# Chunk 8 of a retention kernel turned by VectorE and ScalarE instead of TensorE

## The chip, the cores and the metric

The kernel runs on one core of a Trainium2 chip. The metric is the device time of one execution in microseconds (us). The kernel before took 932.46 us (median of 3 runs, 931.74 to 933.03). A core has five engines that work side by side, each through a queue of its own: TensorE (PE; its weight loads are listed as PEld), VectorE (DVE), ScalarE (ACT), GpSimd (POOL) and SyncE (SP, which here only issues transfers).

## The reference: what is computed

Retention without a normalisation, for 8 batches, 8 heads, 576 positions and 64 channels per head, and then a feed-forward layer with a squared ReLU over the 4608 tokens of 512 channels:

```python
def _attn_ref(q, k, v):
    scores = scale * np.matmul(q, k.transpose(0, 1, 3, 2))
    gamma = 1.0 - 2.0 ** (-5.0 - np.arange(H))
    rel = pos[:, None] - pos[None, :]
    Dmat = np.where(rel >= 0, gamma[:, None, None] ** rel[None, :, :], 0.0)
    return np.matmul(scores * Dmat[None], v)

x = attn_out.transpose(0, 2, 1, 3).reshape(B * S, H * D)
h = np.maximum(x @ w_in, 0.0)          # w_in: 512 x 2048
out = h * h @ w_out                    # w_out: 2048 x 512
```

All of it is in fp32. The weights come as 64-bit numbers and are rounded to fp32 on the chip.

## The kernel before

**Tiles and stages.** The 4608 tokens are cut into 36 chunks of 128 (C) and 9 blocks of 512 (TOK), four chunks to a block. The decay is split into a factor of q and one of k/v, so a chunk needs its scores, a mask, the product with v, and a running state u that is carried from half chunk to half chunk (64 rows; 9 halves make a sequence). The results go to xT, transposed, which the feed-forward layer reads. The first layer of block 0 is plain products (`first_in`, 16 steps of 8 matrix products each); the blocks after it use a scheme of seven products (`ffn_in`). The second layer follows once all chunks are done.

**The order is written by hand.** The main loop runs i from 5 to 36. In turn i it finishes chunk i - 1 (`whole(i - 1)`, which also makes the scores of chunk i), prepares the transposed q and k of a later chunk, issues loads, and runs some steps of the feed-forward layer (`ffn(i - 1)`). While block 0 lasts (i = 5 to 8), `ffn` runs 3 steps, called a, b and c here. Each has a few copies (`move`), the six instructions of rounding one piece of weights (`convert(6)`: L227, L231, L238, L241 and L244 on VectorE, L235 on ScalarE between them), one entry of the list `flips`, and one `first_in`, whose eviction is L683 on ScalarE and whose squaring L685 is issued one step later, before the next L683. Engines take their work in the order of issue.

**Two ways to transpose q and k of a chunk.** Up to chunk N_TURN - 1, `turn` does it on TensorE: `turn_in` makes 16 transposes (L445) into two PSUM banks, `turn_out` copies these to the tile qk (L454, two copies of 128 x 512, here both on ScalarE). From chunk N_TURN on, `flip` does it in advance: two entries of `flips` with one VectorE transpose each in squares of 32 (L416; k first, then q), the second of which also puts 16 copies of 32 x 256 into the list `moves`. `move(count)` then issues up to `count` of these on ScalarE (L431), which puts the squares in their places. A move of block 0's turns can be issued from the step after the one that listed it.

**What whole(i) asks of ScalarE.** After the first products of the state (first group of L568) ScalarE copies the state out of PSUM (`grown`, L501). TensorE goes on with half of the scores of chunk i + 1 (L480) and the carry products (L609, 32 of them, or 16 where a sequence begins within the chunk), and then adds to the same PSUM bank (second group of L568). At its end ScalarE copies the result to xT (`x_out`, L550) and the state again (L501).

**Scaling.** q and v of each chunk are scaled in place by GpSimd (`scale_q`, L396, and `scale_v`, L495), in the order of issue. How far ahead scale_q runs depends on N_TURN too (the last lines of the loop below). Buffers: 3 tiles of q, 5 of k, 4 of v, 3 of qk, 2 of flip, 3 PSUM banks for `first_in`.

```python
    for i in range(N_EARLY + 1, N_CH + 1):
        move(C, i)
        whole(i - 1)
...
        if i + 1 < N_TURN:
            turn(i + 1, (0, 0))
...
        if N_TURN <= i + 2 < N_CH:
            flip(i + 2)
        ffn(i - 1)
        for j in range(n_scaled[0], min(i + (4 if i > N_TURN - 4 else 3), N_CH)):
            n_scaled[0] += 1
            scale_q(j, nc.gpsimd)
```

Of the kernel before, what the change touches and what calls it, by code (L numbers as in the profile page):

```python
# [41 lines left out]
def kernel(  # L42
# [290 lines left out]
    def convert(count):  # L333
        for _ in range(count):
            f = next(w_in_steps, None)
            f and f()
# [61 lines left out]

    N_TURN = 9
    ps_t = [None]
    moves = []

# [7 lines left out]
    def flip(i):  # L412
        t = work2.tile([128, 4, 2, HP, 32], F32, tag="flip", name="flip")

        def one(j):
            nc.vector.transpose(t[:, :, j, :, :], loaded[i][j].rearrange("s (p e) (d a) -> s (e d) p a", e=2, d=2))  # L416

        def two():
            one(0)
            to = new_qk(i)  # L420
            for b in range(C // 32):
                for g in range(4):

                    moves.append((i, done[0] + (1 if steps[0][0] == 0 else 2), to[32 * g:32 * g + 32, :, :, 32 * b:32 * b + 32], t[32 * b:32 * b + 32, g, :, :, :]))

        flips.extend([lambda: one(1), two])

    def move(count, i=N_CH):

        while moves and count and moves[0][0] <= i and (moves[0][1] <= done[0] or count == C):  # L430
            nc.scalar.copy(*moves.pop(0)[2:])  # L431
            count -= 1
# [23 lines left out]
    def turn(i, engines=(0, 1)):  # L456
        turn_in(i)
        turn_out(i, engines)
# [338 lines left out]
    def step():  # L797
        n, f, *args = steps.pop(0)
        done[0] += 1
        f(*args)  # L800
        for _ in range(2 if len(transfers) > 2 else 1):
            if transfers and ahead[0] > QUIET:
                transfers.pop(0)[1]()
# [9 lines left out]
    def ffn(i):  # L813

        if steps and steps[0][0] == 0:

            for _ in range((N_W1 - N_EARLY) * C // TOK):
                move(4)
                convert(6)
                for f in flips[:1]:  # L820
                    f()
                del flips[:1]
                step()
            return
        count = N_MP * NP * C // TOK
        while steps and count:
            held[0] = count <= 1

            due = sum(m[0] <= i + 2 for m in moves)
            move(max(2, min(4, -(-due // (count - 1)))) if count > 1 else 0)  # L830
            ahead[0] = count
            busy[0] = len(flips) > 0
            for f in flips[:1]:
                f()
            del flips[:1]
            step()
            count -= 1
        held[0] = busy[0] = False
        ahead[0] = N_DF
# [7 lines left out]
    def loads(i):  # L847
        if i + 3 < N_CH:
            load(i + 3, "qk")
        if i + 2 < N_CH:  # L850
            load(i + 2, "v")
# [63 lines left out]
# [3 lines that stand above are left out]
        if i == N_EARLY + 1:  # L918
            convert(4)
        if i + 1 < N_TURN:  # L920
            turn(i + 1, (0, 0))
        if i + 1 < N_CH:
            scale_v(i + 1)
        loads(i)
# [6 lines that stand above are left out]
# [296 lines left out]
```

## Time and profile before

| | before |
|---|---|
| median of 3 runs | 932.46 us (931.74 to 933.03) |
| the profiled execution, its own time | 931.4 us |
| its span, first to last instruction | 929.7 us |
| granted TensorE clock | 0.999 |
| turn i = 6 (chunk 5 finished), turn i = 7, turn i = 8 | 53.88 to 67.14, 67.14 to 80.41, 80.41 to 93.03 us |
| transposes of TensorE, L445 | 144, the last ones at 69.3 to 69.9 us |
| copies of them, L454 | 15 on ScalarE (591 ns median), 3 on VectorE (691 ns) |
| VectorE transposes, L416 | 54, 702 ns median, from 73.1 us on |
| copies into place, L431 | 432, 402 ns median, from 77.6 us on |

A profile is taken of one execution; the time of that execution is somewhat longer than the span of its instructions. "Busy" is the time in which an engine has an instruction running. A line of a timeline has the start, the duration, the engine, the line of the kernel, the operation, what is written and read with its shape, and how many such instructions it sums up; in square brackets stands the idle time of the engine before it and what ended it. A line of the chain of waits in order of time has start, duration, engine and line of one piece of the work that leads to the end. Durations of matrix products overlap[...], so they don't add up; the distance between starts does.

### The profile page before, as it was taken

To read this page: it belongs to the slowest core of one execution; us is meant where nothing else is said; L and a number is where in the kernel's file an instruction comes from. 1 tells how busy PE (TensorE), PEld (TensorE's weight loads), DVE (VectorE), ACT (ScalarE), POOL (GpSimd) and SP (SyncE) were. 2 spreads that over 40 slices of the span, in tenths; PEclk is the share of its full clock that TensorE was granted. 3 is DMA by queue.
4 is the path that set the end of the run, shared out by engine and by line. 5 is a ranking of instruction groups with operands and counts; after the bars stand their busy time and mean duration, and the time that the engine had idled before them with its cause. 6 is when DMAs were issued, how large, how long until landed. Compare 5 with 4: busy or idle time off the path is not lost.

```text
span 929.7 us, 21073 instructions
## 1 busy us (share of the span) xinstructions
PE 922.7 (99%) x8548; PEld 830.3 (89%) x8548; DVE 756.2 (81%) x1215; ACT 346.4 (37%) x788; POOL 84.3 (9%) x84
## 2 busy tenths in 40 slices
PE   8999999999999999999999999999999999999998
PEld 7654888888888888888888899999999999999997
DVE  5888798888898888979876587878888888877887
ACT  3457767667676676676711110000000000000000
POOL 3322111121111111211000000000000000000000
PEclk9999999999999999999999999999999999999999
DMA  9998657678666785784379996566666575465523
GB/s 223 223 258 231 169 150 200 165 212 267 166 182 182 261 216 146 224 267 140 115 255 345 381 334 194 145 165 197 175 165 195 151 209 156 116 177 138 151 85 68
DMA packets 297152, 181.29 MB, mean 195 GB/s; under 512 B 194112, under 2 KB 270016, under 8 KB 296160
## 3 DMA queue, kind: packets, MB, share of 16 engines
q1 hardware_dynamic: 292064, 178.81, 66.4%
q10 hardware_dynamic: 4928, 1.08, 0.6%
q8 instruction: 67, 1.10, 0.5%
q14 instruction: 29, 0.24, 0.1%
q0 software_dynamic: 64, 0.07, 0.0%
HBM read 109.39 MB, written 70.52 MB: 194 GB/s over the span
## 4 chain that ended last, share of the span: by engine, by line
PE 98%; DVE 1%; issue 0%; POOL 0%; ACT 0%; POOLq 0%; DVEq 0%
PE h_b L717 18%; PE o_b L1063 17%; PE h_a L717 12%; PE h_c L717 12%; PE o_c L1063 12%; PE o_a L1063 12%; PE h_ps L677 6%; PE x_ps L574 3%; PE sc_ps L480 2%; PE x_ps L609 1%; PE u_ps L568 1%; PE idle_ps L845 0%; PE t_ps L445 0%; PE sc_ps L509 0%; PE x_ps L535 0%; DVE room L513 0%
## 5 line engine op out<-in xcount | busy, mean ns | idle before, releaser
L717 PE MATMUL h_b<-room,w 128*128 128x256 f32 x768 | 181.5, 379 | 0.0
L431 ACT COPY qk<-flip 32x256 f32<-32x256 f32 x432 | 173.8, 402 | 6.7
L717 PEld LDWEIGHTS h_b<-room,w 128*128 128x128 f32 x768 | 145.8, 190 | 20.0 <-DVE room L736 0.2
L717 PE MATMUL h_a<-room,w 128*128 128x256 f32 x512 | 123.9, 385 | 0.0
L717 PE MATMUL h_c<-room,w 128*128 128x256 f32 x512 | 121.0, 379 | 0.0
L717 PEld LDWEIGHTS h_c<-room,w 128*128 128x128 f32 x512 | 97.3, 190 | 13.2
L717 PEld LDWEIGHTS h_a<-room,w 128*128 128x128 f32 x512 | 95.0, 190 | 13.7
L1063 PE MATMUL o_b<-room,w 128*128 128x192 f32 x496 | 90.7, 326 | 0.0
L1076 ACT COPY r<-o_a 128x192 f32<-128x192 f32 x28 | 8.9, 319 | 209.4 <-PE o_a L1063 209.4
L1063 PEld LDWEIGHTS o_b<-room,w 128*128 128x128 f32 x496 | 82.3, 190 | 0.0
L724 DVE SCALAR_TENSOR_TENSOR room<-room 128x512 f32<-128x512 f32 x96 | 67.2, 700 | 3.3
L396 POOL TENSOR_TENSOR q_ld<-q_ld,dv 128x512 f32<-128x512 f32 x34 | 37.8, 1113 | 286.2 <-DMA q_ld<-in_q_dram 240.7
L1063 PE MATMUL o_a<-a,w 128*128 128x192 f32 x352 | 62.6, 326 | 0.0
L1063 PE MATMUL o_b<-s,w 128*128 128x192 f32 x336 | 61.5, 326 | 0.0
L1063 PE MATMUL o_c<-s,w 128*128 128x192 f32 x336 | 61.5, 326 | 0.0
L1063 PE MATMUL o_c<-room,w 128*128 128x192 f32 x336 | 61.5, 326 | 0.0
L677 PE MATMUL h_ps<-room,w 128*128 128x512 f32 (+1 forms) x152 | 57.7, 532 | 0.6 <-DVE w L244 0.5
L1063 PEld LDWEIGHTS o_a<-a,w 128*128 128x128 f32 x352 | 58.1, 190 | 0.1
L1063 PE MATMUL o_a<-room,w 128*128 128x192 f32 x320 | 56.9, 326 | 0.0
L1063 PEld LDWEIGHTS o_b<-s,w 128*128 128x128 f32 x336 | 55.8, 190 | 0.0
L1063 PEld LDWEIGHTS o_c<-s,w 128*128 128x128 f32 x336 | 55.8, 190 | 0.0
L1063 PEld LDWEIGHTS o_c<-room,w 128*128 128x128 f32 x336 | 55.8, 190 | 0.0
(117 smaller groups left out, 1412.6 us busy)
## 6 DMA issues: line engine op xcount, KB each, us to landing
g_dram<-room SPq DMA_DIRECT2D x164, 256.0 KB, 3.8
a<-g_dram SPq DMA_DIRECT2D x30, 512.0 KB, 5.8
room<-g_dram SPq DMA_DIRECT2D x28, 512.0 KB, 5.1
w_dram<-w SPq DMA_DIRECT2D x28, 448.0 KB, 4.4
w<-w_dram SPq DMA_DIRECT2D x7, 1792.0 KB, 9.6
q_ld<-in_q_dram SPq DMA_DIRECT2D x64, 128.0 KB, 4.1
w<-in_moe_w_in_dram SPq DMA_DIRECT2D x16, 512.0 KB, 6.0
w<-in_moe_w_out_dram SPq DMA_DIRECT2D x64, 128.0 KB, 3.4
```

Source lines behind the costliest of these rows:

```text
L396: engine.tensor_tensor(t, t, dv[:, heads, at:at + 1].to_broadcast(list(t.shape)), op=ALU.mult)
L431: nc.scalar.copy(*moves.pop(0)[2:])
L480: nc.tensor.matmul(st[i]["sc"][e][rows(h), hp, :], lhsT=st[i]["kT"][rows(e), hp, t], rhs=st[i]["qT"][rows(e), hp, t], start=True, stop=Tru ...
L568: return [lambda hp=hp, e=e, b=b: nc.tensor.matmul(u[rows(e), hp, :], lhsT=loaded[i][1][rows(h), 2 * hp + e, :], rhs=st[i]["vs"][rows(h), ...
L574: return [lambda hp=hp, e=e, b=b: nc.tensor.matmul(x_at(hp, e, b, h), lhsT=s["vs"][rows(h), head(hp, e), :], rhs=s["ret"][rows(h), e, hp, ...
L609: m = nc.tensor.matmul(x_at(hp, e, b, h), lhsT=u[rows(e), hp, :], rhs=s["qT"][rows(e), hp, CH * h:CH * h + CH], start=clears(b, e), stop=F ...
L677: nc.tensor.matmul(p, lhsT=w[:, c, :], rhs=xT[0][:, c, :].rearrange("p (h t) -> p h t", h=2)[:, lo:hi, at[0]:at[1]], start=(c == 0), stop= ...
L717: nc.tensor.matmul(p[:, mm, :], lhsT=w[:, c, :], rhs=xs[n][right][:, c, :], start=(j in OPENS and mm == 0 and c == 0), stop=(j in CLOSES a ...
L724: nc.vector.scalar_tensor_tensor(t, t, 0.0, t, op0=ALU.max, op1=ALU.mult)
L1063: nc.tensor.matmul(p, lhsT=w_out[j][:, m, WO_SLOT[right], :], rhs=s["lefts"][left][:, m, :], start=(i in OPENS and m == 0), stop=(i in CLO ...
L1076: nc.scalar.copy(r[:, 0, LEFT], p)
```

## The change

N_TURN goes from 9 to 8: chunk 8 is now transposed by `flip(8)` in turn i = 6 (its two VectorE transposes stand in steps a and b, its first copies in step c) instead of by `turn(8)` in turn i = 7. In the turns of block 0 up to 5 copies are issued in a step where it was 4. As the bound of the scaling loop also reads N_TURN, scale_q(8) is issued in turn 5 instead of turn 6.

```diff
-    N_TURN = 9
+    N_TURN = 8
...
             for _ in range((N_W1 - N_EARLY) * C // TOK):
-                move(4)
+                move(5)
                 convert(6)
                 for f in flips[:1]:
                     f()
```

## The prediction

> **What bounds the kernel now.** I read the busy shares and the chain of waits on the page first, then the chain in order of time around the first block, then a table of engine time by turn of the main loop, and last the timelines of ScalarE (ACT), VectorE (DVE) and TensorE (PE) there.
>
> ```profile
> PE 922.7 (99%) x8548; PEld 830.3 (89%) x8548; DVE 756.2 (81%) x1215; ACT 346.4 (37%) x788; POOL 84.3 (9%) x84
> ...
> PE 98%; DVE 1%; issue 0%; POOL 0%; ACT 0%; POOLq 0%; DVEq 0%
> ```
>
> PE sets the end: whatever delays or frees PE goes into the time almost one to one. ACT is at 37% over the whole span, but that is no guide here, since it is idle after 480 us. The place of the change is 54 to 93 us, turns i = 6, 7 and 8:
>
> ```profile
> core 0: us, PE busy (x) PEld busy (x) DVE busy (x) ACT busy (x) POOL busy (x), PEclk, DMA share, GB/s
> 53.88:67.14 13.26, 13.26 (x169) 7.11 (x168) 12.05 (x18) 7.58 (x15) 3.32 (x3) 1.00 0.96 267
> 67.14:80.41 13.27, 13.27 (x170) 7.11 (x169) 9.27 (x18) 8.99 (x18) 2.02 (x2) 1.00 0.92 261
> 80.41:93.03 12.62, 12.62 (x154) 6.53 (x153) 11.87 (x17) 10.31 (x23) 5.18 (x6) 1.00 0.82 195
> ```
>
> PE is full in all three turns, and the two turns that hold 16 transposes are 0.65 us longer than the third. The chain in order of time has the same:
>
> ```profile
> 69.28 0.06 PE u_ps L568 x3
> 69.34 0.64 PE t_ps L445 x16
> 69.98 10.50 PE h_ps L677 x24
> ...
> 82.54 0.06 PE u_ps L568 x3
> 82.60 10.50 PE h_ps L677 x24
> ```
>
> The transposes of chunk 8 (L445) stand bare between two other pieces of PE work: 0.64 us.
>
> The third thing is how close PE is to waiting for ACT. In whole(i), ACT copies the running state out of PSUM (`grown`, L501), and PE may add to that bank again (second group of L568) only when the copy is done. Timeline, whole(4) and then whole(6):
>
> ```profile
> 41.37 0.41 PE L609 MATMUL x_ps<-qk,u_sb 64*64 64x64 f32 x16
> 41.38 0.37 ACT L501 COPY u_sb<-u_ps 128x256 f32<-128x256 f32 x1
> 41.90 0.27 PE L568 MATMUL u_ps<-v_ld,k_ld 64*64 64x64 f32 x2
> ...
> 67.89 0.65 PE L609 MATMUL x_ps<-qk,u_sb 64*64 64x64 f32 x32
> 67.91 0.37 ACT L501 COPY u_sb<-u_ps 128x256 f32<-128x256 f32 x1
> 68.42 0.27 PE L568 MATMUL u_ps<-v_ld,k_ld 64*64 64x64 f32 x2
> ```
>
> whole(4) has 16 carry products (L609) where whole(6) has 32, yet L568 follows the start of whole after 1.27 us in both (40.63 to 41.90, 67.15 to 68.42) and 0.14 to 0.15 us after the end of L501. So in whole(4) PE does wait for the copy, and with 32 products the slack is some 0.05 us at most. If ACT comes to L501 late, PE stands still by the same amount.
>
> And ACT comes to it just in time in turn i = 8, after the first four copies of chunk 9 (timeline):
>
> ```profile
> 76.67 0.70 DVE L416 STREAM_TRANSPOSE flip<-q_ld 128x512 f32<-128x512 f32 x1
> 77.08 0.60 ACT L683 ACTIVATE room<-h_ps 128x512 f32<-128x512 f32 x1 [1.65 <-PE h_ps L677]
> 77.58 1.63 ACT L431 COPY qk<-flip 32x256 f32<-32x256 f32 x4
> 79.23 0.72 ACT L235 ACTIVATE w<-w,exp_bias 128x512 uint32<-128x512 uint32 x1
> 79.86 0.61 ACT L685 ACTIVATE room<-room 128x512 f32<-128x512 f32 x1
> 80.51 0.60 ACT L683 ACTIVATE room<-h_ps 128x512 f32<-128x512 f32 x1
> 81.17 0.37 ACT L501 COPY u_sb<-u_ps 128x256 f32<-128x256 f32 x1
> ```
>
> L683 at 80.51 starts exactly when its products are done (the first of that turn was 3.74 us after PE began, and each step is 3.43 us: 69.91 + 3.74 + 6.86 = 80.51). L501 at 81.17 is also on time. There is nothing left over.
>
> [...] L501 never passes an L683 or an L431 issued before it. [...] L431 has 402 ns[...]. [...] Here L231 takes 1.28 us beside the GpSimd scaling at 56.80 us, and 0.42 us otherwise; the transposes L416 (671 to 705 ns, all 54) show no such growth.
>
> **The change part by part.**
>
> *PE, turn 7.* turn(8) is gone: 16 transposes, -0.64 us, all on the path. Their PSUM banks are not short (L677 shows no wait).
>
> *ACT and DVE.* Two copies L454 (1.09 us) leave turn 7. Two L416 enter turn 6 (steps a and b of three; 0.62 us each from start to next start, as at 76.67 to 77.30). 16 L431 enter, 0.41 us each: 5 in step c of turn 6, 5 in a, 5 in b and 1 in c of turn 7. Then chunk 9's copies follow with 4 in c of turn 7, 5, 5 and 2 in turn 8, and 3 of chunk 10. So turns 6, 7, 8 get 5, 15, 15 copies where they had 0, 4, 12. In turn 7 one step on ACT is now 5 x 0.41 + L235 0.63 + L685 0.52 + L683 0.55 (start to next start) = 3.76 us, against 3.43 us of PE.
>
> *GpSimd.* The condition i > N_TURN - 4 lets scale_q(8) be issued one turn earlier, ahead of scale_v(7). Its q was issued by SP at 46.58 us and lands in about 4 us, so the 1.06 us at 56.80 moves to about 52. Nothing is added; the 0.86 us it cost L231 moves into turn 5, where DVE has 0.56 us idle before L491. I take DVE to be about 0.5 us earlier in turn 6 for it (bounds 0 to 0.86).
>
> *Turn 6.* DVE ended step b at 63.49 us. With two transposes (+1.24) and 0.5 earlier, the flip of chunk 8 ends near 64.2 (64.9 without the gain). ACT is free after L683 of step b at 63.82 + 0.53 = 64.35. Five copies: L235 at 66.42, L685 at 67.05, L683 at 67.57 (before: 67.25), L501 at 68.13 instead of 67.91. PE stalls 0.2; if the flip comes at 64.9 and is seen by 65.05, it is 0.9. I take 0.3.
>
> *Turn 7*, counted from x_out (L550) of whole(6): two copies L501/L550 0.8; five L431 to 2.86; L235, L685, L683 start at 2.86, 3.49, 4.03 (PE is ready at 3.7); five L431 from 4.6; L235 of step b at 6.66, ends 7.38. DVE's third pass of step b (L241) has been waiting for that L235: L241 7.41, L244 8.14, and only behind these in its queue the transpose of chunk 9's q, 8.75 to 9.45. ACT, which did L683 and the last copy of chunk 8 by 8.85, waits for it: four L431 from 9.55, L235 11.2, L685 11.85, L683 12.4, L501 12.95. In the trace of before that L501 is 11.26 us after PE began h_ps, so 11.2 from x_out. Late by 1.75 us (1.55 to 2.0, from the start-to-start gaps 0.5 to 0.66 after L683 and 0.75 to 0.87 after L550), and PE stalls by it in whole(7).
>
> *Turn 8 and after.* L501 isn't called in whole(8) in this place, for chunk 8's second half ends a sequence; five copies without L235 in steps b and c (2.06 + 0.63 + 0.55 = 3.2 us) fit beside 3.43 of PE. From turn 9 on the instructions are the same, but for three fewer copies left. Weights: step c of turn 7 needs a piece converted in its step a, which ends near 5.0, and PE comes to it at 6.8; covered. The SP queue's loads and the stores of g come up to 2 us later and are needed 8 us or more later; 0.
>
> *Sum:* -0.64 + 0.3 + 1.75 = +1.4 us. Against the profiled execution: span 929.7 to 931.1, its own time 931.4 to 932.8. The median of the runs shown is 932.46, 1.1 above that execution; with the same difference 933.9.
>
> **Rivals.** An effect of 0.2% (1.86 us) is about what a measurement of this kernel can tell from no change.
>
> (A) Forecast: both stalls as worked out, net +0.7 to +1.8. For it: the two copies L501 on time to 0.05 us. Chance 0.44.
>
> (B) The flip of chunk 8 comes late in turn 6, because DVE isn't freed by the earlier scaling or is held by another GpSimd pass in step a or b. Place: the L431 of step c, turn 6. Price: each 0.1 us past 64.35 is 0.1 us of stall; at 65.05 it gives -0.64 + 0.9 + 1.75 to 2.0 = +2.0 to 2.3, 934.5 to 934.8. It decides from copies starting after 64.8. For it: DVE has 12.05 us busy of 13.26 there. Against: part of that is overlap of records, and it idles 1.94 us before L491 at 69.16. Chance 0.36; and 0.07 for slower still, where lateness reaches a bank or a load that I count as covered.
>
> (C) The stalls aren't passed on, PE having other work to pull ahead: -0.64, 931.8. Against it stands whole(4). Chance 0.05.
>
> (D) ACT is late by its own queue only, as chunk 9's flip isn't behind L244 in effect: then L501 comes 0.7 to 1.1 us earlier in turn 7, net about +0.5, 933.0. Chance 0.05. That the change doesn't do what it says I hold excluded: turn is guarded by i + 1 < N_TURN alone. A gain of over 1.86 us has no source in the trace, 0.03 for what I don't see.
>
> **Numbers.** No measurable change: A, C, D, 0.54; slower 0.43; faster 0.03. Range 932.3 to 935.6: D's end to B with 1 us of scatter between runs (931.74 to 933.03). The likeliest case alone: 933.1 to 934.3.
>
> **What would show it.** t_ps x128 instead of x144 matrix products; 448 L431; L445 absent near 69 us; in the waits of PE two stalls before the second group of L568, near 68.4 (0.2 to 0.9) and near 81.7 us (about 1.75), each 0.14 us after an L501; in turn 7 ACT without idle time before L683, and DVE idle 2 us before L241 of step c. Wrong would be: L501 on time in whole(7), or PE going on without it, or a loss after 95 us.

## The result, and the profile after

The changed kernel takes 933.18 us (median of 20 runs, 932.58 to 934.92), the kernel before, run beside it, 931.76 us (20 runs, 931.31 to 933.03): ratio 1.0016, 95% interval 1.0010 to 1.0023. That is 1.4 us slower, as worked out. The interval lies above 1, so the loss is real, and it is smaller than the 0.2% that the prediction took as the least effect that can be told. The span of the profiled execution goes from 929.7 to 931.0 us.

The times fall in two groups: 16 runs from 932.58 to 933.65 us and 4 from 934.23 to 934.92. The profiled execution (932.70 us) is of the lower group, so what follows is the account of that one.

The same view as before, engine time by turn (each turn counted from the first matrix product of its whole):

```profile
core 0: us, PE busy (x) PEld busy (x) DVE busy (x) ACT busy (x) POOL busy (x), PEclk, DMA share, GB/s
53.91:67.18 13.27, 13.27 (x170) 7.11 (x169) 11.46 (x19) 9.01 (x19) 3.12 (x2) 1.00 1.01 269
67.18:80.13 12.95, 12.85 (x154) 6.66 (x153) 10.30 (x16) 10.97 (x25) 2.12 (x2) 1.00 0.94 262
80.13:94.45 14.32, 12.85 (x153) 6.66 (x153) 12.40 (x18) 11.93 (x28) 5.27 (x5) 1.00 0.75 169
```

Turn 7 is 0.32 us shorter than before (12.95 against 13.27), turn 8 is 1.70 us longer (14.32 against 12.62) and TensorE isn't busy for 1.47 us of it. So 0.64 us were saved, and 0.32 and 1.70 lost; whole(8) begins 1.42 us later than before (94.45 against 93.03), and after it nothing more is lost: the span ends 1.3 us later.

The timeline of TensorE at the second group of L568, where both losses are, with ScalarE's copy of the state ahead of it, in whole(6) and in whole(7):

```profile
68.28 0.36 ACT L501 COPY u_sb<-u_ps 128x256 f32<-128x256 f32 x1
68.78 0.27 PE L568 MATMUL u_ps<-v_ld,k_ld 64*64 64x64 f32 x2
...
82.65 0.36 ACT L501 COPY u_sb<-u_ps 128x256 f32<-128x256 f32 x1
83.11 0.27 PE L568 MATMUL u_ps<-v_ld,k_ld 64*64 64x64 f32 x2 [1.47 <-POOL v_ld L495]
```

whole(6) began at 67.19 us and whole(7) at 80.14 us (first L568), so the second group comes after 1.59 and 2.97 us where it was 1.27: stalls of 0.32 and 1.70 us. In both it follows the end of L501 by 0.10 to 0.14 us.

But the profile names another culprit for the second: L495, the scaling of a v by GpSimd. So does the chain of waits in order of time, which leaves TensorE there and runs back for tens of us through loads that bound nothing:

```profile
76.72 4.30 DMA v_ld<-in_v_dram
81.02 0.07 issue
81.09 1.31 POOL v_ld L495
82.40 0.71 issue
83.11 0.27 PE u_ps L568 x2
```

The reader should be wary of the 0.71 us of "issue" between the supposed releaser and the released: from the end of L501 to the second group of L568 it was 0.10 to 0.15 us in every case shown, here and in the prediction. By order of issue this L495 is also that of chunk 9's v, which whole(7) doesn't read. Which of the two it was is the first thing that the experiments decide.

How ScalarE came to be late in turn 7 (timeline; the lines of VectorE that it waits for are put between):

```profile
69.67 0.59 ACT L550 COPY room<-x_ps 128x512 f32<-128x512 f32 x1 [1.03 <-PE x_ps L574]
...
74.42 2.07 ACT L431 COPY qk<-flip 32x256 f32<-32x256 f32 x5
76.52 0.72 ACT L235 ACTIVATE w<-w,exp_bias 128x512 uint32<-128x512 uint32 x1
77.28 0.69 DVE L241 SCALAR_TENSOR_TENSOR w<-w,w 128x512 f32<-128x512 f32 x1 [0.43 <-ACT w L235]
78.00 0.69 DVE L244 SCALAR_TENSOR_TENSOR w<-w,w 128x512 uint32<-128x512 uint32 x1
78.61 0.70 DVE L416 STREAM_TRANSPOSE flip<-q_ld 128x512 f32<-128x512 f32 x1
...
79.35 1.65 ACT L431 COPY qk<-flip 32x256 f32<-32x256 f32 x4 [0.68 <-DVE flip L416]
81.02 0.72 ACT L235 ACTIVATE w<-w,exp_bias 128x512 uint32<-128x512 uint32 x1
81.65 0.62 ACT L685 ACTIVATE room<-room 128x512 f32<-128x512 f32 x1
82.17 0.58 ACT L683 ACTIVATE room<-h_ps 128x512 f32<-128x512 f32 x1
```

It is a loop through two engines. Five copies on ScalarE (2.07 us) hold back L235, which starts 0.03 us after the last of them ends; L241 on VectorE waits 0.43 us for L235; the transpose of chunk 9's q stands behind L241 and L244 in VectorE's queue and starts at 78.61 us, after both; and ScalarE, which had caught up, waits 0.68 us for that transpose.

### The profile page after: what moved, and what is told of

Its sections match the earlier page's. It is cut to its first block, busy times and chain, and to the rows that moved or that the text cites. A ratio compares the mean times of both kernels' runs of the same rounds, so it can differ in the third digit from the quotient of the medians.

```text
span 931.0 us, 21058 instructions
## 1 busy us (share of the span) xinstructions
PE 922.5 (99%) x8532; PEld 830.0 (89%) x8532; DVE 759.0 (82%) x1217; ACT 352.2 (38%) x802; POOL 85.6 (9%) x84
## 4 chain that ended last, share of the span: by engine, by line
PE 94%; DMA 2%; SPq 2%; DVE 1%; POOL 0%; issue 0%; ACT 0%; POOLq 0%; DVEq 0%
PE h_b L717 18%; PE o_b L1063 17%; PE h_a L717 12%; PE h_c L717 12%; PE o_c L1063 12%; PE o_a L1063 12%; PE h_ps L677 3%; PE x_ps L574 3%; SPq L158 2%; PE sc_ps L480 1%; DMA v_ld<-in_v_dram 1%; PE x_ps L609 1%; PE u_ps L568 1%; DMA k_ld<-in_k_dram 1%; POOL v_ld L495 0%; PE sc_ps L509 0%
## 5 line engine op out<-in xcount | busy, mean ns | idle before, releaser
L431 ACT COPY qk<-flip 32x256 f32<-32x256 f32 x448 | 180.5, 403 | 8.8 <-DVE flip L416 1.8
```

## The experiments

Two theories were set against each other. S: ScalarE comes late to L501, and TensorE stands still by as much. G: TensorE waits in whole(7) for the v that GpSimd scales. In this table "stall" is the time from the first L568 of a whole to its second group, less the 1.27 us of before; all times in us. The stalls and spans are those of one profiled execution. The ratio comes from all runs and is not the quotient of the two medians; where some runs lie far above the others (e5, e9) it is the higher of the two.

| kernel | stall whole(5), (6), (7) | span of the profile | median | before beside it | ratio (95% interval) |
|---|---|---|---|---|---|
| before | 0, 0, 0 | 929.7 | - | 931.76 | - |
| changed | 0, 0.32, 1.70 | 931.0 | 933.18 | 931.76 | 1.0016 (1.0010 to 1.0023) |
| e1: N_TURN = 8, move(4) | 0.65, 0, 0; 1.9 in whole(8) | 931.8 | 933.44 | 931.65 | 1.0020 (1.0010 to 1.0031) |
| e2: N_TURN = 9, move(5) | 0, 0, 0.30 | 930.1 | 931.86 | 931.65 | 1.0002 (0.9994 to 1.0010) |
| e3: copies fitted | 0, 0, 0 | 929.0 | 930.90 | 931.65 | 0.9994 (0.9986 to 1.0003) |
| e4: transpose first | 0, 0.08, 1.03 | 929.9 | 932.25 | 931.65 | 1.0005 (0.9997 to 1.0013) |
| e5: scaling put back | 0.22, 1.20, 1.69 | 932.6 | 932.88 | 931.62 | 1.0022 (1.0014 to 1.0030) |
| e6: N_TURN = 7 | 2.64, 0.52, 0.16 | 933.8 | 935.68 | 931.62 | 1.0046 (1.0034 to 1.0059) |
| e7: e3, transpose first, scaling put back | 0, 0, 0 | 928.8 | 930.68 | 931.62 | 0.9992 (0.9985 to 0.9998) |
| e8: scaling early alone | 0, 0, 0 | 929.8 | 931.48 | 931.62 | 1.0001 (0.9993 to 1.0010) |
| e9: e6, transposes of turn 5 later | 1.94, 0, 0 | 931.1 | 932.70 | 931.39 | 1.0019 (1.0011 to 1.0026) |

**e1 and e2: each half of the change alone.** e1 has the first line of the diff only, e2 the second only (`move(4)` to `move(5)` with N_TURN = 9).

> N_TURN = 8 alone, with move(4) as before. Theory S (ScalarE comes late to L501 and TensorE stands still by as much): four copies in a step just fit, so both stalls before the second group of L568 (0.33 us in whole(6), 1.70 us in whole(7)) go to under 0.1 us. But chunk 9 then has only 12 copies in turn 8, and 4 are left for the start of turn 9, behind the last L683: TensorE waits for them at the scores of chunk 9 (L480) in whole(8) by about 1.9 us. Net -0.64 + 1.9 = +1.3 us against before, ratio 1.0014, with the loss near 94 us instead of near 82. Theory G (TensorE waits in whole(7) for the v scaled by GpSimd, L495, as the profile names it): the load and scaling order is that of the changed kernel, so the 1.7 us before L568 in whole(7) stay.

> move(5) alone, N_TURN = 9. Theory S: one copy more (0.41 us) before L501 in step c of turn 7, where nothing is left over: a stall of 0.4 us in whole(7), span 0.4 us longer than before, ratio 1.0004. Theory G: no change in the order of loads and scalings, 0.

In e1 both stalls are gone, and the loss is where S has it, at the scores of chunk 9 in whole(8) (timeline of TensorE):

```profile
93.07 0.62 PE L574 MATMUL x_ps<-qk,v_ld 64*64 64x64 f32 x13
...
94.66 0.32 PE L480 MATMUL sc_ps<-qk 64*64 64x64 f32 x2 [0.81 <-ACT qk L431]
95.50 0.38 PE L480 MATMUL sc_ps<-qk 64*64 64x64 f32 x9 [0.51 <-ACT qk L431]
95.67 0.23 PE L609 MATMUL x_ps<-qk,u_sb 64*64 64x64 f32 x3
```

L609 comes 2.60 us after the start of whole(8), 0.69 before: 1.9 us, as expected. The median is 0.5 us over the expectation; the profile has 0.65 us more in whole(5), which nobody had in the sum (see e5 and e8). Theory G, by which the 1.7 us in whole(7) should have stayed, fails here already.

e2 shows a stall of 0.30 us where 0.41 had been expected, but not for the reason given. ScalarE and TensorE in e2 (timelines):

```profile
77.79 2.06 ACT L431 COPY qk<-flip 32x256 f32<-32x256 f32 x5
79.88 0.72 ACT L235 ACTIVATE w<-w,exp_bias 128x512 uint32<-128x512 uint32 x1
81.50 0.36 ACT L501 COPY u_sb<-u_ps 128x256 f32<-128x256 f32 x1
82.01 0.27 PE L568 MATMUL u_ps<-v_ld,k_ld 64*64 64x64 f32 x2
```

The copies began 0.2 us later than before (77.79 against 77.58), and with one copy more L235 began 0.65 us later (79.88 against 79.23). That the transpose of chunk 9's q held these copies is an estimate: they began 0.69 us after L683 (77.10), where it was 0.50 before, and the copies of the changed kernel that waited for a transpose began 0.03 and 0.04 us after its end (64.53 to 64.56, 79.31 to 79.35), which puts the end of this one near 77.75 us. L501 came only 0.33 us later (81.50 against 81.17), since 1.62 us instead of 1.94 passed between the two. So ScalarE had some 0.3 us in hand in that step before the change. An estimate from these lines: the one copy, with the transpose on time, would stall TensorE by 0.41 - 0.3, about 0.1 us; no run shows it alone. The span grows by 0.4, and the medians (0.2 us apart) can't tell that from nothing.

Together: with N_TURN = 8 chunk 9 needs more than four copies a step somewhere before whole(8), and five in every step are what overloads turn 7.

**e3: the copies where ScalarE has room.**

```diff
-            for _ in range((N_W1 - N_EARLY) * C // TOK):
-                move(5)
+            for j in range((N_W1 - N_EARLY) * C // TOK):
+                move((5, 6, 5)[j] if i == 7 else 4)
```

> N_TURN = 8 with 4 copies a step in turns 6 and 7 and 5, 6, 5 in the three steps of turn 8, where whole(8) has no L501 in this place and chunk 9 needs its 16 copies done before its scores. Theory S: no stall in whole(6), whole(7) or whole(8) over 0.1 us, so only the saving is left: -0.64 us against before, ratio 0.9993. Theory G: the 1.7 us in whole(7) stay, net about +1.1 us, ratio 1.0011.

No stall is left, and the span is 0.7 us under that of before. The medians are 0.75 us apart, but the interval still holds 1. G falls here too. ScalarE, TensorE and GpSimd in turn 8 of e3 (timelines):

```profile
80.60 0.37 ACT L501 COPY u_sb<-u_ps 128x256 f32<-128x256 f32 x1
81.07 0.24 PE L568 MATMUL u_ps<-v_ld,k_ld 64*64 64x64 f32 x1
...
83.64 1.30 POOL L495 TENSOR_TENSOR v_ld<-v_ld,dv 128x512 f32<-128x512 f32 x1 [0.96 <-DMA v_ld<-in_v_dram]
```

TensorE goes on at 81.07 us, before the scaling that the profile had named even begins. With the 0.10 us after L501 in the changed kernel, and with e4 below, the releaser there was L501.

**e4: the loop through VectorE opened.** The changed kernel with one exchange:

```diff
-                convert(6)
                 for f in flips[:1]:
                     f()
                 del flips[:1]
+                convert(6)
                 step()
```

> The changed kernel with the VectorE transpose of a step issued before its convert(6) instead of after. Theory S with the loop through L235 (the transpose of chunk 9's q waits behind L241, which waits for an L235 behind five copies): ScalarE's 0.68 us without work before chunk 9's first copies goes, L501 in turn 8 comes 0.7 us earlier, the stall in whole(7) falls from 1.70 to about 1.0 us, that in whole(6) from 0.33 to about 0.2. Net about +0.55 us against before, ratio 1.0006. If lateness came from the number of copies alone: no change from the changed kernel, +1.4 us. Theory G: +1.4 us too.

ScalarE and TensorE in turn 8 of e4, whose whole(7) began at 79.67 us (timelines):

```profile
77.78 2.08 ACT L431 COPY qk<-flip 32x256 f32<-32x256 f32 x5
81.51 0.36 ACT L501 COPY u_sb<-u_ps 128x256 f32<-128x256 f32 x1
81.97 0.27 PE L568 MATMUL u_ps<-v_ld,k_ld 64*64 64x64 f32 x2 [0.80 <-issue]
```

The stall in whole(7) falls from 1.70 to 1.03 us, by 0.67 for the 0.68 us that ScalarE had waited; in whole(6) 0.08 is left. The median is 0.6 us over before (interval -0.3 to +1.2). Of the 1.70 us, 0.67 was the loop; the rest goes with the number of copies, since e1, with four in a step, has no stall there.

**e5 and e8: GpSimd's order.** e5 is the changed kernel with chunk 8's q scaled behind chunk 7's v, e8 the kernel before with that scaling early.

```diff
+        if N_TURN <= i + 2 < 9:
+            n_scaled[0] += 1
+            scale_q(i + 2, nc.gpsimd)
         loads(i)
...
-        for j in range(n_scaled[0], min(i + (4 if i > N_TURN - 4 else 3), N_CH)):
+        for j in range(n_scaled[0], min(i + (4 if i > 5 else 3), N_CH)):
```

```diff
-        for j in range(n_scaled[0], min(i + (4 if i > N_TURN - 4 else 3), N_CH)):
+        for j in range(n_scaled[0], min(i + (4 if i > 4 else 3), N_CH)):
```

> The changed kernel with the scaling of chunk 8's q put back behind that of chunk 7's v on GpSimd (issued in turn 6, still ahead of flip(8)). Theory S: the reordering, which the step for GpSimd took as free, has a price that differs from run to run: in the profiled run of e1 the scaling at 51.78 us held back an L244, so L227, L235, L683 and L501 came late and TensorE stood still by 0.66 us in whole(5). With the order of before that can't happen: no stall in whole(5), highest minus lowest time at most 1.4 us (2.3 in the changed kernel). In turn 6 the scaling holds up L231 again, so the flip of chunk 8 ends about 0.3 us later and the stall in whole(6) is 0.5 to 0.7 us instead of 0.33; whole(7) 1.7 as before. Median +1.5 to +1.8 us, ratio 1.0017. If the order of the scalings played no part: as the changed kernel in scatter and in both stalls.

> The kernel before with only the scaling of chunk 8's q issued one turn earlier, as the change does. Theory S: no TensorE work changes; where the scaling meets the convert of step c in turn 5[...], L501 in whole(5) is late, 0 to 0.7 us by run. Median +0.0 to +0.4 us, ratio 1.0002, highest minus lowest larger than before's 1.3 us. If the order of the scalings is free: 0 and the same scatter.

e5 is a miss in part. Its median is 1.3 us over before (1.5 to 1.8 expected). Its times scatter more, not less (932.19 to 935.06), whole(5) has 0.22 us of stall, and whole(6) 1.20 us where 0.5 to 0.7 had been expected. VectorE's timeline of turn 6 shows why:

```profile
56.58 1.27 DVE L227 TENSOR_SCALAR w<-w 128x512 uint32<-128x512 uint32 x1
57.77 1.28 DVE L231 TENSOR_SCALAR w<-w 128x512 uint32<-128x512 uint32 x1
...
64.74 0.70 DVE L416 STREAM_TRANSPOSE flip<-q_ld 128x512 f32<-128x512 f32 x1
```

Both scalings (56.51 and 57.53 us) met a pass of VectorE that usually takes 0.42 us; the transpose of chunk 8's q ended at 65.44 instead of 64.53 us, and the copies, L683 and L501 followed it. This is rival B of the prediction, in a kernel that has its condition; this execution took 934.27 us, so it is one of the slower of e5's. (Some 0.5 us of what its span lost arises later than that: the first L568 of whole(8) came 2.33 us later than before, 96.57 against 94.24, and the span is 2.9 us longer.) e8 shows that the early scaling alone costs nothing that can be measured in the kernel before (931.48 against 931.62, scatter 1.5 us). In e1 it did cost 0.65 us in one execution: there the scaling at 51.78 us stretched an L244 to 1.57 us, and L227, L235, L683 and L501 of the same step came late. In the changed kernel the same scaling met an L231, behind the L227 that L235 waits for, and whole(5) had no stall. So the cost of such a meeting depended on what it hit.

The two groups of times of the changed kernel are there in e1, e5 and e9 too (2 of 8, 5 of 13 and 5 of 17 runs above 934 us, the others up to 933.5 us), and not in e2, e3, e4, e7 and e8. That such meetings, and so rival B, make the upper group fits e5's profile, but no other execution of an upper group was profiled: it stays open.

**e7: a version ahead of both.** e3, with the exchange of e4 and the scaling of e5.

> As e3 (4 copies a step in turns 6 and 7; 5, 6, 5 in turn 8), with the transposes issued before convert(6) and chunk 8's q scaled behind chunk 7's v. Theory S: no stall in whole(5) to whole(8) over 0.1 us, -0.64 us, ratio 0.9993, with the scatter of before (highest minus lowest at most 1.4 us).

930.68 us (21 runs), ratio 0.9992 with an interval below 1. That is 0.9 us under the kernel before that ran beside it, where the changed kernel was 1.4 us over. Of the 0.9 us, 0.64 is the saving; the rest isn't explained and is within the interval (0.2 to 1.4 us). No stall is over 0.1 us. The scatter is 1.7 us, a little more than expected.

**e6 and e9: one chunk further.** N_TURN = 7 on top of e7, with two copies behind L501 in whole(5) to whole(7), four a step in turns 5 to 7 and 5, 5, 4 in turn 8; e9 issues the transposes of turn 5 behind convert(6).

```diff
-    N_TURN = 8
+    N_TURN = 7
...
             grown(i, 1)
+            move(2 if i < 8 else 0)
...
+                move((5, 5, 4)[j] if i == 7 else 4)
```

> One chunk further: N_TURN = 7, so chunks 7 and 8 leave TensorE; copies spread so that ScalarE always comes to L501 in time (2 right behind L501 in whole(5) to whole(7), where it waits for TensorE anyway, 4 a step in turns 5 to 7, then 5, 5, 4), transposes issued before convert(6), chunk 7's and 8's q scaled behind the v before it. Theory S: two times 0.64 us saved, no stall over 0.1 us: -1.3 us, ratio 0.9986. If VectorE, fuller by two transposes in turn 5, delays L227 and so L235 and L501 there, a stall of up to 0.7 us in whole(5): -0.6 us, ratio 0.9994. Theory G (the wait is for the scaled v): a stall of about 1.5 us in whole(7) whatever the copies, so 0 or slower.

> As e6, but in turn 5 the transposes of chunk 7 are issued behind convert(6) again. In e6 the transpose of chunk 7's k waited 2.30 us for its transfer and held the convert behind it in VectorE's queue, so L235, L683 and L501 came late. If that transfer was the cause of e6's loss, most of its +4 us goes: the wait falls to under 0.3 us, what is left is VectorE's two transposes more in turn 5 (1.24 us against some 0.6 us idle there): a stall of 0.3 to 0.7 us in whole(5) and up to 0.5 in whole(6), so -0.1 to -0.7 us against before, ratio 0.9993 to 0.9999. If VectorE is too full for chunk 7 wherever its transposes stand, the loss stays over +1.5 us.

Both miss. In e6 the transpose of chunk 7's k, at the head of VectorE's queue, waited for its transfer, and the convert with L235 waited behind it (VectorE's timeline):

```profile
47.88 0.71 DVE L416 STREAM_TRANSPOSE flip<-k_ld 128x512 f32<-128x512 f32 x1 [2.30 <-DMA k_ld<-in_k_dram]
```

TensorE waited 1.26 us for the weights of that convert (turn 5 took 14.76 instead of 13.26 us, which the stalls of the table don't hold), and then for L501 in whole(5). The transfer was not all of it: two scalings of GpSimd (54.18 and 55.19 us) met an L244 and the L227 ahead of that L235 (1.48 and 1.28 us instead of 0.69 and 0.42).

In e9 the wait for the transfer fell to 0.39 us and in the steps of turn 5 no scaling held VectorE up ahead of that L235, so e9 doesn't separate the two. It loses 1.3 us against before where e6 lost 4.1, but doesn't gain: ScalarE's first copies of chunk 7 in turn 5 now wait for the transpose of q.

```profile
53.91 1.65 ACT L431 COPY qk<-flip 32x256 f32<-32x256 f32 x4 [1.49 <-DVE flip L416]
```

L501 stands behind them and comes at 57.21 us in a whole that began at 54.51: 1.94 us of stall. With 1.28 us saved that makes 0.7; in this execution another 0.6 us was lost before whole(4) began (41.24 instead of 40.63 us). It is the mechanism of whole(7) once more; the expectation had counted VectorE's lateness there only by way of L235, and not the copies that wait in ScalarE's queue. In neither of the two places tried did VectorE have chunk 7's transposes done in time; no other was tried.

## Why the prediction was right

The time and the mechanism were forecast: TensorE saves its transposes, ScalarE comes late to L501 in whole(6) and whole(7), and TensorE stands still by as much. Some of the steps in between were off and made up for each other.

**The saving.** The 16 transposes took 0.64 us together. e3 and e7 have the saving bare: turn 7 goes from 13.27 to 12.62 us (67.23 to 79.85 in e3).

**The stalls.** Predicted 0.3 and 1.75 us, measured 0.32 and 1.70. The steps, counted from L550 of whole(6), with the forecast in brackets: L235 3.00 (2.86), L683 4.15 (4.03), second five copies 4.75 (4.6), L241 7.61 (7.41), transpose of chunk 9's q 8.94 to 9.64 (8.75 to 9.45), its copies 9.68 (9.55), L501 12.98 (12.95). Each step up to the copies was 0.1 to 0.2 us late, and the gap from L683 to L501 was shorter than taken (0.48 against 0.55), so the errors cancelled in part.

**"There is nothing left over."** This reading of turn 8 was wrong by some 0.3 us. L683 waited there for its products and L501 for TensorE, and when ScalarE is late these waits go: e2 shows L235 0.65 us later and L501 only 0.33. The sum for turn 7 was not hurt, since it counted the steps at their shortest distances, as they are when ScalarE is late.

**GpSimd and turn 6.** Here the right stall came in part by luck. The scaling moved to 52.55 us as said, but the gain for VectorE was 0.17 us (L244 of step a ended at 60.40 instead of 60.57) where 0.5 had been taken: VectorE was held at L231 (1.31 us) and L244 (1.43 us) in turn 5 and came to L491 at 56.80 instead of 55.90. (At its old place, 56.80 us, the scaling had taken 1.24 us, not the 1.06 of the prediction.) The transpose ended at 64.53 us (64.2 forecast). The other end of that forecast, 64.9 without the gain, was a slip too: 63.49 + 1.24 is 64.73. The copies began at 64.56 instead of 64.35 us, which by the prediction's own price (0.2 us of stall at 64.35 and 0.1 for each 0.1 after it) is 0.4 us; L235 to L501 took 1.63 us instead of the 1.71 counted, which leaves about the 0.32 measured. The 0.3 of the prediction was its 0.2 moved up a little toward the 0.9 of the bad case, and so it hit although the gain behind it was a third of what was taken.

**Turn 8 and later.** No stall in whole(8), none after: 1.42 us at its start, 1.3 at the end. ScalarE waited 1.10 us for the transpose of chunk 10 in step c, which hadn't been counted, and which nothing of TensorE was behind.

**The rivals.** A is what the profiled execution shows. B didn't happen there (its copies start at 64.56, before 64.8), but e5 shows it, and the four runs of the upper group may be cases of it, which isn't shown: they are 2.5 to 3.2 us over the kernel before, where B had been priced at 2.0 to 2.3. C falls with all runs, since TensorE passes each late L501 on (second group of L568 0.10 to 0.15 us after its end); D is refuted by e4, which puts a size of 0.67 us on the loop.

**The signs.** 128 transposes, 448 copies, ScalarE without idle time before L683, both stalls in place. Two were named wrongly: VectorE's long wait was before the L241 of step a (1.82 us), not of step c (0.30), and the profile's list of waits has one of the stalls, under GpSimd's name.

**The base.** The three runs shown had a median of 932.46; over 20 runs it is 931.76, so the forecast of 933.9 stood 0.7 us too high, with the difference right.

## What to carry to other kernels

Before work is taken off the engine that bounds, find the waits of that engine that are met with nothing to spare, and ask what the replacement puts ahead of the instruction that ends them: here saving 0.64 us of TensorE put 16 copies of 0.41 us into the queue of an engine busy 37% of the span, and each L501 issued behind them ran behind them, 0.37 us (68.28 against 67.91) and 1.48 us (82.65 against 81.17) later than before. Spread such filler by the room in each step and keep it away from the step before a hand-over; the same 16 copies cost 2.0 us or nothing, by where they stood. Where a chain of waits leaves the bounding engine with a long "issue" behind it, look for another instruction that ended just before the wait did (0.10 to 0.15 us here).

## What the runs showed that was not expected

- GpSimd's 128 x 512 pass beside VectorE cost 0.7 to 0.9 us for the pass that it met, in the meetings named here (L227 and L231 1.27 to 1.31 instead of 0.42, L244 1.43 to 1.57 instead of 0.69). The same scaling, meeting another pass, cost TensorE nothing in one execution and 0.65 us in another. What holds the pass up isn't shown by the traces.
- The sequence L235, L685, L683, L501 takes 1.63 us from start to start when ScalarE is late (81.02 to 82.65) and 1.94 us when it waits for TensorE (79.23 to 81.17, before the change). The difference is what ScalarE had in hand.
- The profile put a wait for ScalarE down to a scaling and, behind it, to transfers: in its chain 2% went to DMA and 2% to SP, and TensorE had 94% where it had 98% before.
